# Two cleared PSUM banks and one counting product moved within the experts of a fused attention and mixture kernel

## The chip, the cores and the metric

The kernel runs on one core of one Trainium2 chip. The metric is the device time of one execution in microseconds (us); a kernel's time is the median of its runs.

## What is computed

The reference has three stages: a linear attention with a decaying state, a dense gated layer, and a mixture of eight experts of which each token uses two.

```python
for t in range(S):                       # 4 x 8 heads, 768 steps, head size 48
    state = alpha[:, :, t, :, None] * state + einsum('bhd,bhe->bhde', k[:, :, t], v[:, :, t])
    y[:, :, t] = einsum('bhd,bhde->bhe', q[:, :, t], state)
x = y as 3072 tokens of 384 columns
x = ((x @ w1) * (x @ w2)) @ w3 @ w_out   # 384 -> 1024 -> 1024 -> 384
logits = x @ w_gate + log1p(exp(x @ w_noise)) * noise
top2, weights = the two greatest of 8 experts per token, softmax over them
for e in range(8):
    h = maximum(x[tokens of e] @ w1[e], 0)          # 384 -> 1024
    out[tokens of e] += weight * (h @ w2[e])        # 1024 -> 384
```

## The kernel before

**Stages.** Attention and the dense layer run over eight groups of 384 tokens. Each group ends in `finish` (norms, tokens written to DRAM) and `route` (the two experts of each token), and later `rank` gives each token a slot in its experts' tables. The slots' addresses are `ad` (L697); GpSimd then writes six scatters into the table in DRAM (L700). The experts follow, and this change lies in their beginning.

**An expert** takes 832 slots in two parts of 512 and 320. For a part, SyncE reads the table (`mt`, L971), GpSimd gathers the tokens (`xg`, L910) and SyncE transposes them (`xT`, L916). The first layer runs in eight units (`first`, f = 0 to 7): nine products into one bank (L922 to L924: value and residue in f16), ScalarE takes the positive part (`hh`, L925), VectorE the residue (`hl`, L926), which also frees the bank. The second layer (`second`) runs in tiles of 128 slots, 24 products each (L932 to L934); ScalarE scales the result with the factors `wv` (L976, VectorE, from the table) and GpSimd adds it to the output (L958).

**The last 64 slots** of an expert are not always filled. `count_few` counts the rows of each expert once: it casts the counts `R` to `rb` (L1011), multiplies with ones on TensorE (L1013) and sets a flag per expert, `more` (L1016 to L1018). TensorE loads the flags (L1127) and branches: only where `more` is set, `first_few` runs 72 small products for the last 64 slots (L1038 to L1040), all eight units into one bank. Without those products the bank must hold zeros, so `cleared` has VectorE clear it beforehand (L1027); the products wait for that.

**Banks.** There are eight PSUM banks. A new tile takes the one that was free first by the scheduler's order, and its writer waits for the last reader of the tile before.

**Order.** The kernel is written as one program; a scheduler then sets the order of ScalarE, VectorE, GpSimd and SyncE from its own estimate of durations, while TensorE keeps the order of the code. Each engine runs its queue in that order.

**Around the change** (`experts`): the eight units of expert 0's first part, `rank` of the last group, `count_few`, four tiles of second layers of expert 0's first part, the eight units of expert 1's first part (a table read and transposes beside them), `first_few(0)`, the eight units of expert 0's second part, its tiles, then the eight units of expert 1's second part with `overflow_plan` (a list of slots beyond 832, small steps on VectorE), and `first_few(1)`. For both, `cleared(NF)` stands after unit 4. Weights come in pieces beside all this: load, greatest magnitude (`esc`, L881, then `em`, L884), a product that spreads it (L889), scales (L893 to L897), and a cut into value and residue (`eh` L180, `el` L184).

Of the kernel before, what the change touches and what calls it, by code (L numbers as in the profile page):

```python
# [8 lines left out]
F32 = mybir.dt.float32  # L9
F32R = mybir.dt.float32r  # L10
F16 = mybir.dt.float16
BF = mybir.dt.bfloat16
# [8 lines left out]
P = 128  # L21
# [3 lines left out]
E = 8  # L25
NK = DM // P
NF = F // P
# [54 lines left out]
def body(ctx, tc, q, k, v, alpha, mw1, mw2, mw3, mwo, wg, wn, noise, ew1, ew2, out, dbg=None):  # L82
    nc = tc.nc
# [28 lines left out]
    R = const.tile([P, E], F32, name="R")  # L112
# [92 lines left out]
    def bank(*shape, dt=F32):  # L205

        t = ps.tile([P, PB], F32, name="ps")
        if dt != F32:
            t = t.bitcast(dt)
        n = 1  # L210
        for x in shape:
            n *= x
        t = t[:, :n]
        return t if len(shape) == 1 else t.rearrange("p (a b) -> p a b", a=shape[0])
# [623 lines left out]
    ep = None  # L838
# [89 lines left out]
    def layer2(w2h, w2l, hh, hl, c0, n, mt, wv, t, midway=None, e=None):  # L928
        ts = slice(c0, c0 + n)
        py = bank(DM)  # L930
        for f in range(NF):
            nc.tensor.matmul(py[:n], hh[:, f, ts], w2h[:, f], start=f == 0, stop=False)  # L932
            nc.tensor.matmul(py[:n], hh[:, f, ts], w2l[:, f], start=False, stop=False)  # L933
            nc.tensor.matmul(py[:n], hl[:, f, ts], w2h[:, f], start=False, stop=f == NF - 1)  # L934
            if f == 2 and midway:
                midway()
        put(py[:n], n, mt, wv, t, e)
# [36 lines left out]
    def factors(mt, n, s1, s2, part):  # L974
        wv = ep.tile([P, NTA], F32, name=f"wv{part}")
        nc.vector.tensor_scalar(wv[:, :n], mt[:, :n, 1], s1[:, 4:5], s2[:, 4:5], op0=OP.mult, op1=OP.mult)  # L976
        return wv
# [9 lines left out]
    def fetch_part(e, p):  # L987
        c0, c1 = PARTS[p]
        t0, nt = c0 // P, -(-(c1 - c0) // P)
        rows = P + NTOK - (NL * G if e < NFR and p == 0 else 0)  # L990
        mt = slots(table[e, :, t0:t0 + nt, :], nt, p)
        xT = ep.tile([P, 2 * NK, nt * P], F16, name=f"xT{p}", bufs=1)
        EX[e, p] = (mt, xT, [gather(mt, t, rows) for t in range(nt)])

    def turn_part(e, p, t):
        mt, xT, xg = EX[e, p]
        turn(xg[t], xT, t)

    def first(e, p, f):
        n = PARTS[p][1] - PARTS[p][0]  # L1000
        if (e, p) not in EH:
            EH[e, p] = [ep.tile([P, NF, n], F16, name=f"h{x}{p}", bufs=1) for x in "hl"]
        if p:
            n = FULL - G0
        layer1(f, EW[e][0], EW[e][1], EX[e, p][1], n, *[h[:, :, :n] for h in EH[e, p]])

    def count_few():

        V = nc.vector
        rb = ep.tile([P, E], BF, name="rb", bufs=1)  # L1010
        V.tensor_copy(rb, R)  # L1011
        pc = bank(E)
        nc.tensor.matmul(pc, ones, rb, start=True, stop=True)  # L1013
        n = ep.tile([1, E], F32, name="nf", bufs=1)
        more = ep.tile([1, E], I32, name="more", bufs=1)
        V.tensor_copy(n, pc[0:1])  # L1016
        V.tensor_tensor(n[:, :NFR], n[:, :NFR], skip[0:1], OP.add)
        V.tensor_scalar(more, n, float(FULL), None, op0=OP.is_gt)  # L1018
        return more
# [5 lines left out]
    def cleared(m):  # L1025
        pm = bank(m, CAP - FULL)
        nc.vector.memset(pm, 0.0)  # L1027
        return pm

    def first_few(e, pm):  # L1030
        n, c0 = CAP - FULL, FULL - G0
        w1h, w1l, xT = EW[e][0], EW[e][1], EX[e, 1][1]
        for _ in only_few(e):
            for f in range(NF):
                fs = slice(f * P, (f + 1) * P)
                for kk in range(NK):
                    xh, xl = [xT[:, k, c0:c0 + n] for k in (kk, NK + kk)]
                    nc.tensor.matmul(pm[:, f], w1h[:, kk, fs], xh, start=kk == 0, stop=False)  # L1038
                    nc.tensor.matmul(pm[:, f], w1h[:, kk, fs], xl, start=False, stop=False)  # L1039
                    nc.tensor.matmul(pm[:, f], w1l[:, kk, fs], xh, start=False, stop=kk == NK - 1)  # L1040
        if (e, 1) not in EH:
            EH[e, 1] = [ep.tile([P, NF, CAP - G0], F16, name=f"h{x}1", bufs=1) for x in "hl"]
        hh, hl = [h[:, :, c0:] for h in EH[e, 1]]
        nc.scalar.activation(hh, pm, AF.Relu)
        nc.vector.scalar_tensor_tensor(hl, pm, 0.0, hh, op0=OP.max, op1=OP.subtract)

    def second(e, p, t, midway=None):
        n = PARTS[p][1] - PARTS[p][0]
        mt = EX[e, p][0]
        if t == 0:  # L1050
            WV[e, p] = factors(mt, -(-n // P), EW[e][2], EW[e][5], p)
        wv = WV[e, p]
        layer2(EW[e][3], EW[e][4], *EH[e, p], t * P, min(P, n - t * P), mt, wv, t, midway, e)
# [40 lines left out]
    def next_weights(e):  # L1094
        a, b = weights_for(e)
        todo.extend(pause(1) + a[2:4] + pause(1) + a[5:10] + b[1:2] + a[10:] + pause(1) + b[2:4] + pause(2) + b[5:])

    def prepare(n):

        if not n or not todo:  # L1100
            return
        with ExitStack() as st:
            for e in (mybir.EngineType.DVE, mybir.EngineType.Activation):
                for i in [i for i in nc.cur_bb.bb.instructions[-60:] if i.engine == e][-1:]:
                    st.enter_context(tc.issue_after(i))
            for _ in range(min(n, len(todo))):
                todo.pop(0)()

    def experts():
        for f in range(NF):  # L1110
            first(0, 0, f)
            prepare((0, 1, 1, 1, 1, 1, 1, 1)[f])
        for t in range(NTP[0]):
            turn_part(1, 0, t)
        rank(NG - 1)
        more = count_few()
        for t in range(NTP[0]):
            second(0, 0, t)
            prepare(2)
            if t == 0:  # L1120
                fetch_part(0, 1)
        for f in range(NF):
            first(1, 0, f)
            prepare(1)
            if 0 < f <= NTP[1]:
                turn_part(0, 1, f - 1)
            MORE[f] = nc.tensor.value_load(more[0:1, f:f + 1])  # L1127
            if f == NF // 2:
                pm = cleared(NF)
        first_few(0, pm)  # L1130
        prepare(len(todo))
        fetch_part(1, 1)
        next_weights(2)
        for f in range(NF):
            first(0, 1, f)
            prepare(f // 4)
        for t in range(NTP[1] - 1):
            turn_part(1, 1, t)
            py = cleared(NK) if t else None
            second(0, 1, t)  # L1140
            prepare(2)
        turn_part(1, 1, NTP[1] - 1)
        li = None
        for e in range(1, E):
            if e > 1:
                for f in range(NF):
                    first(e, 0, f)
                    if f == 0:
                        rest = last_few(e - 1, py)
                    if f == 1:  # L1150
                        rest()
                    if f == NF // 2:
                        pm = cleared(NF)
                    prepare(1)
                first_few(e, pm)
            if e + 1 < E:
                fetch_part(e + 1, 0)
            for f in range(NF):
                first(e, 1, f)
                if f == 0 and e == 1:  # L1160
                    rest = last_few(0, py)
                    li = overflow_plan()
                if f == 1 and e == 1:
                    rest()
                if e == 1 and f == NF // 2:
                    pm = cleared(NF)
                prepare(1)
            if e == 1:
                first_few(1, pm)
            if e + 1 < E:  # L1170
                fetch_part(e + 1, 1)
            for t in range(NTP[0]):
                second(e, 0, t)
                prepare(2)
                if e + 1 < E:
                    turn_part(e + 1, 0, t)
            prepare(len(todo))
            if e + 2 < E:
                next_weights(e + 2)
            if e < E - 1:  # L1180
                for t in range(NTP[1] - 1):
                    turn_part(e + 1, 1, t)
                    py = cleared(NK) if t else None
                    second(e, 1, t)
                turn_part(e + 1, 1, NTP[1] - 1)
        py = cleared(NK)
        second(E - 1, 1, 0)
        rest = last_few(E - 1, py)
        second(E - 1, 1, 1, rest)
        return li  # L1190
# [137 lines left out]
```

## Time and profile before

| | us |
|---|---|
| median of 3 runs (lowest, highest) | 947.82 (943.57, 949.92) |
| the profiled execution's own time | 936.92 |
| its span, first to last instruction | 935.1 |
| TensorE busy | 897.5 (96%) |
| VectorE busy | 624.3 (67%) |
| ScalarE busy | 447.6 (48%) |
| GpSimd busy | 259.6 (28%) |

Times in the profile are from the start of the span. PE is TensorE, DVE VectorE, ACT ScalarE, POOL GpSimd, SP SyncE. A row of a timeline has the start, the duration, the engine, the line, the operation with its output and input tiles, and in brackets the idle time before it and what ended it. Matmuls are pipelined: the next one starts before the one before has ended, so the pace is the distance of the starts.

### The profile page before, as it was taken

To read this page: it belongs to the slowest core of one execution; us is meant where nothing else is said; L and a number is where in the kernel's file an instruction comes from. 1 tells how busy PE (TensorE), PEld (TensorE's weight loads), DVE (VectorE), ACT (ScalarE), POOL (GpSimd) and SP (SyncE) were. 2 spreads that over 40 slices of the span, in tenths; PEclk is the share of its full clock that TensorE was granted. 3 is DMA by queue.
4 is the path that set the end of the run, shared out by engine and by line. 5 is a ranking of instruction groups with operands and counts; after the bars stand their busy time and mean duration, and the time that the engine had idled before them with its cause. 6 is when DMAs were issued, how large, how long until landed. Compare 5 with 4: busy or idle time off the path is not lost. (4 is left out here: it accounts for less than half of the span.)

```text
span 935.1 us, 17673 instructions
## 1 busy us (share of the span) xinstructions
PE 897.5 (96%) x6824; PEld 600.0 (64%) x6824; DVE 624.3 (67%) x1733; ACT 447.6 (48%) x916; POOL 259.6 (28%) x246
## 2 busy tenths in 40 slices
PE   7779999999999999999999998999999999999997
PEld 4667777777767666576766455765656564657574
DVE  6899888578788789697769855635555555555320
ACT  2586666364475655754546433334344343434321
POOL 1311110003041131414132243442333333343203
PEclk9889899999999999999999999999999999999999
DMA  9889572241504434101128247585868777776303
GB/s 239 234 148 149 144 200 75 35 93 55 116 10 109 62 102 69 44 26 44 61 83 180 94 87 193 123 165 105 188 122 174 136 155 155 153 157 137 39 10 48
DMA packets 189274, 105.63 MB, mean 113 GB/s; under 512 B 156912, under 2 KB 174912, under 8 KB 189184
## 3 DMA queue, kind: packets, MB, share of 16 engines
q1 hardware_dynamic: 172624, 68.04, 34.2%
q0 software_dynamic: 16560, 36.37, 18.1%
q8 instruction: 59, 0.97, 0.4%
q14 instruction: 31, 0.25, 0.1%
HBM read 73.06 MB, written 20.31 MB: 100 GB/s over the span
## 5 line engine op out<-in xcount | busy, mean ns | idle before, releaser
L958 POOL DMA_INDIRECT out_dram<-ysb,mt x56 | 87.6, 1564 | 151.6 <-ACT ysb L955 147.4
L922 PE MATMUL ps<-xT,eh 128*128 128x256 f16 (+1 forms) x384 | 125.1, 326 | 2.1 <-DVE hl L926 0.9
L934 PE MATMUL ps<-eh,hl 128*128 128x384 f16 x384 | 125.2, 326 | 0.0
L933 PE MATMUL ps<-el,hh 128*128 128x384 f16 x384 | 125.2, 326 | 0.0
L932 PE MATMUL ps<-eh,hh 128*128 128x384 f16 x384 | 125.1, 326 | 0.0
L924 PE MATMUL ps<-xT,el 128*128 128x256 f16 (+1 forms) x384 | 125.1, 326 | 0.0
L923 PE MATMUL ps<-xT,eh 128*128 128x256 f16 (+1 forms) x384 | 125.1, 326 | 0.0
L926 DVE SCALAR_TENSOR_TENSOR hl<-ps,hh 128x512 f16<-128x512 f32 (+1 forms) x128 | 69.7, 552 | 78.8 <-ACT hh L925 78.4
L955 ACT ACTIVATE ysb<-ps,wv 128x384 f32<-128x384 f32 (+1 forms) x56 | 32.4, 579 | 137.9 <-PE ps L934 83.9
L925 ACT ACTIVATE hh<-ps 128x512 f16<-128x512 f32 (+1 forms) x128 | 62.3, 489 | 73.8 <-PE ps L924 65.1
L700 POOL DMA_INDIRECT table<-md,ad x48 | 51.1, 1065 | 154.9 <-DVE ad L697 126.7
L184 DVE SCALAR_TENSOR_TENSOR el<-es,esc,eh 128x512 f16<-128x512 f32 (+1 forms) x80 | 66.7, 851 | 37.8 <-ACT eh L180 37.8
L910 POOL DMA_INDIRECT xg<-x2s,mt x56 | 56.6, 1011 | 95.0 <-DMA mt<-table 59.8
L545 ACT ACTIVATE ab<-ps 128x384 f32<-128x384 f32 (+2 forms) x136 | 63.0, 471 | 36.3 <-PE ps L543 20.8
L182 POOL TENSOR_TENSOR sm<-sf,sm 128x512 f16<-128x512 f32 x24 | 29.8, 1271 | 153.4 <-ACT sm L180 153.4
L541 PE MATMUL ps<-xT,w1h 128*128 128x384 f16 (+2 forms) x204 | 65.2, 321 | 0.9 <-DVE Kt L246 0.6
L541 PE MATMUL ps<-xT,w0h 128*128 128x384 f16 (+2 forms) x204 | 64.9, 320 | 0.9 <-ACT xT L408 0.9
L570 PE MATMUL ps<-Wh,gh 128*128 128x400 f16 x192 | 63.9, 333 | 1.3 <-ACT gh L180 1.1
L543 PE MATMUL ps<-xT,w1l 128*128 128x384 f16 (+2 forms) x204 | 65.1, 320 | 0.0
L542 PE MATMUL ps<-xT,w1h 128*128 128x384 f16 (+2 forms) x204 | 65.1, 320 | 0.0
L543 PE MATMUL ps<-xT,w0l 128*128 128x384 f16 (+2 forms) x204 | 65.0, 320 | 0.0
L542 PE MATMUL ps<-xT,w0h 128*128 128x384 f16 (+2 forms) x204 | 65.0, 320 | 0.0
(303 smaller groups left out, 2083.5 us busy)
## 6 DMA issues: line engine op xcount, KB each, us to landing
es<-in_moe_w_dram SPq DMA_DIRECT2D x32, 768.0 KB, 5.5
s<-in_moe_w_dram POOLq DMA_DIRECT2D x16, 512.0 KB, 4.9
out_dram<-zero POOLq DMA_DIRECT2D x5, 960.0 KB, 5.2
v<-in_v_dram SPq DMA_DIRECT2D x24, 192.0 KB, 2.7
x2s<-xr SPq DMA_DIRECT2D x24, 192.0 KB, 1.9
pad<-in_alpha_dram SPq DMA_DIRECT2D x21, 192.0 KB, 4.0
pad<-in_q_dram SPq DMA_DIRECT2D x21, 192.0 KB, 5.0
pad<-in_k_dram SPq DMA_DIRECT2D x21, 192.0 KB, 4.9
```

Source lines behind the costliest of these rows:

```text
L184: nc.vector.scalar_tensor_tensor(lo, src, scale, hi, op0=OP.mult, op1=OP.subtract)
L541: nc.tensor.matmul(pm, wab[i][0][:, kk, fs], xT[:, kk, cs], start=kk == 0, stop=False)
L542: nc.tensor.matmul(pm, wab[i][0][:, kk, fs], xT[:, NK + kk, cs], start=False, stop=False)
L543: nc.tensor.matmul(pm, wab[i][1][:, kk, fs], xT[:, kk, cs], start=False, stop=kk == NK - 1)
L922: nc.tensor.matmul(pm, w1h[:, kk, fs], xT[:, kk, :n], start=kk == 0, stop=False)
L923: nc.tensor.matmul(pm, w1h[:, kk, fs], xT[:, NK + kk, :n], start=False, stop=False)
L924: nc.tensor.matmul(pm, w1l[:, kk, fs], xT[:, kk, :n], start=False, stop=kk == NK - 1)
L926: nc.vector.scalar_tensor_tensor(hl[:, f], pm, 0.0, hh[:, f], op0=OP.max, op1=OP.subtract)
L932: nc.tensor.matmul(py[:n], hh[:, f, ts], w2h[:, f], start=f == 0, stop=False)
L933: nc.tensor.matmul(py[:n], hh[:, f, ts], w2l[:, f], start=False, stop=False)
L934: nc.tensor.matmul(py[:n], hl[:, f, ts], w2h[:, f], start=False, stop=f == NF - 1)
L958: i = nc.gpsimd.indirect_dma_start(out=out, out_offset=bass.IndirectOffsetOnAxis(ap=mt[:n, t, 0:1].bitcast(U32), axis=0), in_=ys[:n], in_o ...
```

## The change

`count_few` takes its operand `rb` from outside and its product is written behind the first tile of expert 0's second layers instead of before it. The bank of the last 64 slots is cleared after unit 1 instead of after unit 4, for expert 0 and for expert 1.

```diff
-    def count_few():
+    def count_few(rb):
 
         V = nc.vector
-        rb = ep.tile([P, E], BF, name="rb", bufs=1)
-        V.tensor_copy(rb, R)
+        n = ep.tile([1, E], F32, name="nf", bufs=1)
         pc = bank(E)
         nc.tensor.matmul(pc, ones, rb, start=True, stop=True)
-        n = ep.tile([1, E], F32, name="nf", bufs=1)
...
         rank(NG - 1)
-        more = count_few()
+        rb = ep.tile([P, E], BF, name="rb", bufs=1)
+        nc.vector.tensor_copy(rb, R)
         for t in range(NTP[0]):
             second(0, 0, t)
+            if t == 0:
+                more = count_few(rb)
...
-            if f == NF // 2:
+            if f == 1:
                 pm = cleared(NF)
         first_few(0, pm)
...
-                if e == 1 and f == NF // 2:
+                if e == 1 and f == 1:
                     pm = cleared(NF)
```

Lines behind the edit shift by one or two: L1038 is L1036 in the changed kernel, L1027 is L1025.

Since the scheduler takes the code anew, VectorE's order moves in more than the named places. At the end of the last group (narrow products, before `route`), the order of VectorE is, as a difference of changed against before; `esc_7088` is the magnitude of expert 1's second weights, `am` the norms of the last group:

```order
 L881 TENSOR_REDUCE esc_7085<-es 128x1 x2
 L884 TENSOR_REDUCE em<-esc_7085 128x1
-L881 TENSOR_REDUCE esc_7088<-es 128x1
 L172 TENSOR_SCALAR am<-am 128x3
 L173 TENSOR_SCALAR am<-am 128x3
```

The reduction of expert 1's second weights no longer stands before the norms. It stands now behind the slots' addresses `ad` of the last rank and the counting steps, which moved there too; `el_7087` is the residue of expert 1's first weights:

```order
 L694 SCALAR_TENSOR_TENSOR rs<-si 128x6
 L697 TENSOR_TENSOR ad<-rs,rr 128x6
+L1014 COPY nf<-ps 1x8
+L1197 CAST rb<-R 128x8
+L1015 TENSOR_TENSOR nf<-nf,skip 1x2
+L1016 TENSOR_SCALAR more<-nf 1x8
+L881 TENSOR_REDUCE esc_7088<-es 128x1
 L184 SCALAR_TENSOR_TENSOR el_7087<-es,esc_7085,eh_7086 128x512
 L881 TENSOR_REDUCE esc_7088<-es 128x1
```

Four counting steps and one reduction now follow `ad`; before, the counting steps stood between the rank's steps. The third place is VectorE beside expert 1's first units, where `hl_7522` is their residue, `el_7090` the residue of expert 1's second weights and `hl_7718` that of expert 0's last 64 slots:

```order
 L926 SCALAR_TENSOR_TENSOR hl_7522<-ps,hh_7521 128x512
 L184 SCALAR_TENSOR_TENSOR el_7090<-es,esc_7088,eh_7089 128x768
+L1025 MEMSET ps 128x512
 L926 SCALAR_TENSOR_TENSOR hl_7522<-ps,hh_7521 128x512
 L184 SCALAR_TENSOR_TENSOR el_7090<-es,esc_7088,eh_7089 128x768
-L926 SCALAR_TENSOR_TENSOR hl_7522<-ps,hh_7521 128x512
-L1027 MEMSET ps 128x512
-L926 SCALAR_TENSOR_TENSOR hl_7522<-ps,hh_7521 128x512 x4
-L1022 UNCONDITIONAL_BRANCH
-L1045 SCALAR_TENSOR_TENSOR hl_7718<-ps,hh_7717 128x8x64
+L926 SCALAR_TENSOR_TENSOR hl_7522<-ps,hh_7521 128x512 x5
```

The clearing stands one residue of the weights and two of the units earlier. For expert 1 it moved in the same way, from behind the steps of `overflow_plan` to behind the second of them. In TensorE's order only the counting product moved. Of the banks, expert 0's cleared one is now that of the counting product; unit 6 of expert 1 waits for ScalarE in both orders, and unit 7 for VectorE.

## Rows read from the trace of the kernel before

**Rows 1.** The page, busy us, share of the span and instructions of each engine.

```profile
PE 897.5 (96%) x6824; PEld 600.0 (64%) x6824; DVE 624.3 (67%) x1733; ACT 447.6 (48%) x916; POOL 259.6 (28%) x246
```

**Rows 2.** Waits of TensorE, 400 to 935 us: total, times, longest.

```profile
PE ps L1038 <- DVE ps L1027: 3.2, 2, 1.7
PE ps L922 <- DVE hl L926: 0.9, 1, 0.9
PE ps L1013 <- DVE rb L1011: 0.7, 1, 0.7
```

**Rows 3.** Timeline of TensorE: start, us, engine, line, operation.

```profile
541.44 0.17 PE L672 MATMUL ps<-M,ones 128*128 128x24 bf16 x1
...
542.34 0.32 PE L932 MATMUL ps<-eh,hh 128*128 128x384 f16 x1
...
554.03 0.17 PE L889 MATMUL ps<-em,part 128*128 128x1 bf16 x1
...
571.34 0.38 PE L924 MATMUL ps<-xT,el 128*128 128x512 f16 x1
572.62 0.38 PE L922 MATMUL ps<-xT,eh 128*128 128x512 f16 x1 [0.90 <-DVE hl L926]
...
574.35 0.38 PE L924 MATMUL ps<-xT,el 128*128 128x512 f16 x1
576.26 0.19 PE L1038 MATMUL ps<-xT,eh 128*128 128x64 f16 x1 [1.54 <-DVE ps L1027]
...
604.25 0.27 PE L924 MATMUL ps<-xT,el 128*128 128x256 f16 x1
606.18 0.20 PE L1038 MATMUL ps<-xT,eh 128*128 128x64 f16 x1 [1.66 <-DVE ps L1027]
...
840.81 0.38 PE L924 MATMUL ps<-xT,el 128*128 128x512 f16 x1
841.03 0.19 PE L1038 MATMUL ps<-xT,eh 128*128 128x64 f16 x1
```

**Rows 4.** Timeline of VectorE.

```profile
526.07 1.75 DVE L881 TENSOR_REDUCE esc<-es 128x1 f32<-128x1536 f32 x1 [0.72 <-DMA es<-in_moe_w_dram]
527.74 0.16 DVE L172 TENSOR_SCALAR am<-am 128x3 int32<-128x3 int32 x1
...
546.35 0.17 DVE L697 TENSOR_TENSOR ad<-rs,rr 128x6 int32<-128x6 f32 x1
...
550.12 0.16 DVE L884 TENSOR_REDUCE em<-esc 128x1 bf16<-128x2 f32 x1
...
569.83 0.29 DVE L976 TENSOR_SCALAR wv<-mt,esc,esc 128x3 f32<-128x3 f32 x1 [11.31 <-DMA mt<-table]
...
571.89 0.68 DVE L926 SCALAR_TENSOR_TENSOR hl<-ps,hh 128x512 f16<-128x512 f32 x1
...
573.41 0.68 DVE L926 SCALAR_TENSOR_TENSOR hl<-ps,hh 128x512 f16<-128x512 f32 x1
...
575.73 0.48 DVE L1027 MEMSET ps<- 128x512 f32 x1
...
605.64 0.48 DVE L1027 MEMSET ps<- 128x512 f32 x1
```

**Rows 5.** Timeline of ScalarE, the last group's sums of squares.

```profile
526.49 0.19 ACT L575 ACTIVATION_READ_ACCUMULATOR xr<-ps 128x1 f32 x1
```

**Rows 6.** Busy by stretch: PE, PEld, DVE, ACT, POOL, granted clock, DMA share, GB/s.

```profile
527.70:546.50 18.80, 18.10 (x95) 8.88 (x93) 17.60 (x87) 8.88 (x18) 0.00 (x0) 1.00 0.17 54
576.00:578.00 2.00, 1.74 (x60) 1.74 (x60) 2.00 (x5) 0.00 (x0) 0.00 (x0) 1.00 0.91 331
```

**Rows 7.** Timeline of GpSimd, the first of the last six scatters.

```profile
546.79 0.95 POOL L700 DMA_INDIRECT table<-md,ad  x1 [24.55 <-DVE ad L697]
```

**Rows 8.** Timeline of SyncE's queue, the read of the table that L976 waits for.

```profile
565.28 0.57 SPq L971 DMA_DIRECT2D mt<-table  x1
```

**Rows 9.** Operations with tile mt, whole run: time to landing.

```profile
DMA to landing us min/median/max: 1.5/4.4/9.9
```

## The prediction

> **What bounds the kernel.** I read the page first: TensorE is busy 96% of the span [rows 1]. So only time in which TensorE stands still can be won. The list of its waits in the second half (from 400 us) came next. It names three places that this change touches: the product on the last 64 rows waiting for its cleared bank (L1038, 3.2 us in 2), one layer-1 product waiting for a bank (L922, 0.9) and the counting product waiting for its operand (L1013, 0.7) [rows 2]. The list counts from the modelled end of the product before; what TensorE loses is the distance between starts beyond the usual one, so I took the timeline for all four. Counting: L672 starts at 541.44, L932 at 542.34; two small products need 0.03 each (60 of them take 1.74 us [rows 6]), so 0.84 is lost. Unit 7 of expert 1 starts at 572.62, where 571.34 + 0.22 = 571.56 was due: 1.06 lost. The last 64 rows of expert 0 start at 576.26 instead of 574.35 + 0.22 = 574.57: 1.69 lost. Those of expert 1 start at 606.18 instead of 604.25 + 0.11 = 604.36 (256 columns, half of the 0.22 for 512): 1.82 lost [rows 3]. That a taken branch costs nothing of its own is seen at a later expert, whose bank was cleared in time: 840.81 to 841.03, the usual 0.22 [rows 3]. After 606 the list of waits has nothing for TensorE.
>
> Why these waits are there is in VectorE's timeline. It runs in order, and at 569.83 it comes out of an 11.31 us wait for one read of the table (the factors of expert 1's second part, L976) [rows 4]. Behind that stood the residues (hl) of all the units that TensorE had finished meanwhile. I call this moment D. Everything TensorE waits for at 572 and 576 comes at a fixed distance behind D: unit 0's residue starts at D + 2.06, and the clearing starts at 575.73, D + 5.90 [rows 4].
>
> **The counting product.** In the changed order it stands behind the 24 products of the first tile, and its operand is cast long before. TensorE starts the second layers 0.84 us sooner, and the product itself (0.03) is only moved. But this gain alone goes no further than unit 7: that unit needs the bank that unit 0's residue frees, which is set by D. Without an earlier D, TensorE would just wait 0.84 longer there. So I enter nothing for it.
>
> The move adds one wait: VectorE's copy of the counts now waits for a product that ends about 545.5 (541.5 plus 24 products of 0.162; 72 of them lie between 542.34 and 554.03). Queued behind it are one reduction of 1.75 us, the residues of expert 1's first weights, another reduction and the maximum `em`, for which TensorE's product L889 waits. Before, `em` starts at 550.12 and L889 at 554.03 [rows 3, 4], so the cover is 3.9 us; L889 comes 0.84 sooner, and the reduction moved here costs up to 1.75 if no idle time takes it. At least 1.3 us of cover stay, so the cost is nothing; past that, each us is one us of TensorE. The loads of the flag on TensorE come ten us later still.
>
> **What the scheduler moved with it.** That reduction stood before the first step of the last group's norms (L172): it ran from 526.07, and L172 could start only at 527.74 [rows 4]. L172 needs ScalarE's sums, which were there at 526.49 + 0.19 = 526.68 [rows 5]. Now it comes first: about 1.0 us sooner. From there to the slots' addresses (L697) VectorE is busy 17.60 of 18.80 us [rows 6], so it sets the pace there, and the residues between the steps don't wait for TensorE; I take the whole 1.0. The four small counting steps that stood among the rank's steps leave too, but fill the gaps between dependent steps, so I give them 0.05. L697 then comes at 546.35 - 1.05 = 545.30. The bounds are 0 (the residues turn out to wait for TensorE) and 1.4 (all four steps count).
>
> From L697 a chain runs to D with no other late input: GpSimd's six scatters start at 546.79 [rows 7], then the first table read, three gathers, three transposes, and the read that ends D, issued at 565.28 [rows 8]. Each waits for the one before. So D moves from 569.83 to 568.78, and unit 7 from 572.62 to 571.57. **Gain 1.05** (bounds 0 and 1.9, where 1.9 is all that TensorE lost at the first two places).
>
> **Clearing of expert 0.** The clearing moves ahead of the residues of units 1 and 2, to where the residue at 573.41 started [rows 4]: it ends at 573.41 - 1.05 + 0.48 = 572.84. TensorE gets there at 571.57 + 1.94 (nine products of 0.216; eight lie between 572.62 and 574.35) = 573.51, with 0.67 to spare. **Gain 1.69.** The clearing itself costs nothing new: the same 0.48 us, placed earlier. It puts unit 1's residue off by 0.48 (ends 573.5); expert 0's next unit, which takes that bank, starts about 575.6 (573.51 + 72 products of 0.029). The bank is held six units longer. It is the counting product's, long free, and the wait of unit 7 is again for unit 0's residue and that of unit 6 again for ScalarE (order of the changed kernel), so no earlier unit runs out of banks. If one did, unit 6 would wait instead, 1.94 us sooner.
>
> **Clearing of expert 1.** VectorE is full of overflow-plan steps, which stood before the clearing at 605.64 [rows 4]. In the new order it comes behind the second of them, some 6 us sooner, while TensorE comes 2.74 sooner. **Gain 1.82.** The plan is put off by 0.48; what reads it is far from its end.
>
> **Sum.** 1.05 + 1.69 + 1.82 = 4.56 us, from 936.92 (the span of 935.1 and 1.8 around it) to 932.4 in the profiled execution. The runs shown have their median at 947.82, 1.2% above it; the stalls are taken to be the same there: 947.82 - 4.56 = **943.3 us**, 0.5% less.
>
> **A rule weighed.** The granted clock is 1.00, the 2.4 GHz level, in the two us right behind the 1.69 us stall, and 60 small products take 1.74 us there, 0.029 each [rows 6]. The Trainium skill, "TensorE: Matmul & The Clock Gate", section "HAM oscillation — how this bites in real kernels", says that a TensorE left idle between products falls to half its clock and runs the next ones so. By that rule each stall removed would also give back the slow products behind it; the trace shows none slow behind these stalls. As a mechanism of this kernel: 72 products of 0.029 at half rate would be 2.1 us more at either place, so 8.8 us and 939.1 in all.
>
> **Rivals.**
> - *D does not move.* Table reads, gathers and transposes fix it, or VectorE's lead is lost to waits for residues. For: the chain passes GpSimd, SyncE and five DMA landings. Against: each starts when the one before ends. Gain 3.51, 944.3 us.
> - *Given back later.* TensorE comes 4.6 us sooner to experts 2 to 7, and a weight load or gather is then late by as much. For: 96% busy, little else can be wrong. Against: no wait of TensorE after 606, and loads are issued when compute frees their buffers, so they move along. 947.8 us.
> - *Slower: the table read lands late.* D is one DMA, and each us that it lands later costs TensorE one. It took 4.55 us (565.28 to 569.83); operations with this tile took up to 9.9 to land, median 4.4 [rows 9]. Scatters and gathers that start a us sooner could meet the weight loads in another place. At 9.9, D is 5.35 late: 0.8 slower, 948.6 us; it decides from 4.56 us late on. Against: the same transfers stand in the same order around it.
> - *The clock at half rate behind the stalls:* 939.1 us; against it the granted clock of the row.
> - That the clearing isn't moved at all is excluded by the order.
>
> **How the numbers follow.** Forecast 0.63, D unmoved 0.16, given back (some or all) 0.13, table read late 0.04, clock 0.04. About 1% is what a measurement of this kernel can tell from no change: 9.5 us, which no case reaches. The three runs spread from 4.3 below to 2.1 above their median. So the forecast's own range is 939.0 to 945.4; with the given-back and the late case it goes up to 948.6, and down it is left, since the clock case lies inside. Faster by over 1% (below 938.3) only by the spread of the runs: 0.05. Slower by over 1%: 0.02. Same: 0.93.
>
> **What would show it.** Right: the two waits of L1038's successor are gone from TensorE's list; the wait of the counting product too; unit 7 of expert 1 still waits about 0.9 for a residue, but starts about 571.6; VectorE leaves its table wait about 568.8; L172 starts about 526.7; TensorE reaches the second product on 64 rows about 601.6, and the span is about 930.5. Wrong: a wait at unit 6 (banks), at L889 (the reduction), in TensorE's list behind 606 (given back), or the wait at the 64 rows renamed to a transpose of their tokens.

## The result

The changed kernel takes 936.13 us (median of 7 runs, 934.74 to 940.63) against 946.45 us (7 runs, 943.57 to 949.92) for the kernel before. The ratio is 0.9899, 95% interval 0.9877 to 0.9922: 1.0% faster, 9.6 us (1 - 0.9899 of 946.45; gains below are worked out in this way). The prediction said 943.3 us, with 939.0 as the lower end of its range; the measured time lies below that end. A second measurement, with 29 runs of the kernel before beside it, gave 939.02 against 946.57 us, ratio 0.9924 (0.9900 to 0.9949), so 7.2 us. The two intervals overlap between 0.9900 and 0.9922; I take the gain to be 7.4 to 9.5 us, where 4.56 us were forecast.

The profile shown of the changed kernel is of an execution of 934.74 us (span 933.0 us, 1.7 us around it). That is only 2.2 us less than the profiled execution of the kernel before (936.92 us). The two profiles show much less of a gain than the timed executions, and that is what had to be explained.

In the page, TensorE's row is almost that of [rows 1]; the other engines' rows hardly moved either.

```profile
PE 898.9 (96%) x6824; PEld 600.8 (64%) x6824; DVE 624.3 (67%) x1733; ACT 448.2 (48%) x916; POOL 258.3 (28%) x246
```

TensorE's waits from 400 to 935 us (total, times, longest), to be held against [rows 2]: the two waits for a cleared bank and the one of the counting product are gone. The wait of unit 7 for a residue (L922) is still there, as the prediction said. A new entry stands at the head, L889.

```profile
PE ps L889 <- DVE em L884: 1.1, 1, 1.1
...
PE ps L922 <- DVE hl L926: 0.6, 1, 0.6
```

Four starts in TensorE's timeline (start, us, engine, line, operation), to be held against [rows 3]. The changed file is shorter by two lines there, so that L1036 is the old L1038.

```profile
543.84 0.32 PE L932 MATMUL ps<-eh,hh 128*128 128x384 f16 x1
...
573.84 0.38 PE L922 MATMUL ps<-xT,eh 128*128 128x512 f16 x1 [0.59 <-DVE hl L926]
...
575.78 0.19 PE L1036 MATMUL ps<-xT,eh 128*128 128x64 f16 x1
...
604.07 0.19 PE L1036 MATMUL ps<-xT,eh 128*128 128x64 f16 x1
```

This execution came 2.38 us later than the other one to the last group (the unchanged products from about 517 us to 541 us stand that much later in its trace). From there on it catches up: the start of the first second layer at 543.84 stands 1.50 behind 542.34, unit 7 at 573.84 stands 1.22 behind 572.62, the last 64 rows of expert 0 at 575.78 stand 0.48 ahead of 576.26, those of expert 1 at 604.07 stand 2.11 ahead of 606.18. So between the two profiles the change is worth 2.38 + 2.11 = 4.49 us. The forecast for that pair was 4.56.

VectorE's timeline of the changed kernel, to be held against [rows 4]:

```profile
529.10 0.17 DVE L172 TENSOR_SCALAR am<-am 128x3 int32<-128x3 int32 x1 [1.47 <-ACT xr L575]
...
571.05 0.29 DVE L976 TENSOR_SCALAR wv<-mt,esc,esc 128x3 f32<-128x3 f32 x1 [11.10 <-DMA mt<-table]
...
574.82 0.48 DVE L1025 MEMSET ps<- 128x512 f32 x1
...
599.15 0.48 DVE L1025 MEMSET ps<- 128x512 f32 x1
...
602.62 0.42 DVE L926 SCALAR_TENSOR_TENSOR hl<-ps,hh 128x256 f16<-128x256 f32 x1 [2.02 <-ACT hh L925]
```

The step L172 now waits for ScalarE (1.47 us) instead of standing behind the reduction, and VectorE's table wait ends at 571.05. The clearing for expert 1 runs at 599.15. The last row is the clue to what follows: 3.5 us behind the clearing VectorE stands 2.02 us for an activation of ScalarE. In the kernel before, the clearing stood behind that wait.

### The profile page after: what moved, and what is told of

It is laid out like the page before. It is cut to its first block, busy times and chain, and to the rows that moved or that the text cites. A ratio compares the mean times of both kernels' runs of the same rounds, so it can differ in the third digit from the quotient of the medians.

```text
span 933.0 us, 17675 instructions
## 1 busy us (share of the span) xinstructions
PE 898.9 (96%) x6824; PEld 600.8 (64%) x6824; DVE 624.3 (67%) x1733; ACT 448.2 (48%) x916; POOL 258.3 (28%) x246
## 5 line engine op out<-in xcount | busy, mean ns | idle before, releaser
L922 PE MATMUL ps<-xT,eh 128*128 128x256 f16 (+1 forms) x384 | 125.0, 326 | 1.8 <-DVE hl L926 0.6
L910 POOL DMA_INDIRECT xg<-x2s,mt x56 | 54.4, 971 | 99.7 <-DMA mt<-table 64.7
```

Of the source, the lines that this page charges most:

```text
L922: nc.tensor.matmul(pm, w1h[:, kk, fs], xT[:, kk, :n], start=kk == 0, stop=False)
```

## The experiments

Each kernel is timed against the kernel before on the same chip; the ratio stands with its 95% interval.

**The kernel before and the changed kernel again.** No edit. The question was whether the moment at which the kernel before was timed was out of the ordinary, or its profiled execution.

> The kernel before once more, unchanged, timed against itself on the chip of the other three runs. Theory A (the four stalls are all there is, 4.56 us, and the 10.3 us that were measured come from the moment at which the kernel before was timed): ratio 1.000 and times near 937 to 940, as its profiled execution (936.92). Theory B (the kernel before loses about 10 us in most executions, and its profiled execution was a lucky one): ratio 1.000, times near 946, and its new trace has some 6 us more of waits or of lower clock than the trace shown, at a place that the run names.

Measured: 946.25 us, ratio 1.0004 (0.9987 to 1.0020); profiled execution 944.90 us, span 943.0 us. TensorE's waits from 400 to 935 us in it:

```profile
PE ps L1038 <- DVE ps L1027: 5.8, 2, 4.2
PE ps L922 <- DVE hl L926: 1.0, 1, 1.0
```

The wait for the cleared bank is 5.8 us instead of the 3.2 of [rows 2], and its longest is 4.2 instead of 1.7. It is the one of expert 1. VectorE there:

```profile
604.69 0.16 DVE L1208 TENSOR_TENSOR_SCAN oc<-oc 1x8 f32<-1x8 f32 x1
606.71 0.42 DVE L926 SCALAR_TENSOR_TENSOR hl<-ps,hh 128x256 f16<-128x256 f32 x1 [1.87 <-ACT hh L925]
...
611.72 0.16 DVE L1222 TENSOR_SCALAR li<-lst 1x44 int32<-1x44 f32 x1
611.98 0.48 DVE L1027 MEMSET ps<- 128x512 f32 x1
```

VectorE stands 1.87 us for the activation of unit 2; behind it stand all the rest of the overflow plan and at last the clearing, at 611.98. TensorE had started the last product of its units at 608.00. ScalarE in the same place:

```profile
603.31 0.39 ACT L925 ACTIVATE hh<-ps 128x256 f16<-128x256 f32 x1 [0.97 <-PE ps L924]
606.29 0.39 ACT L925 ACTIVATE hh<-ps 128x256 f16<-128x256 f32 x1 [2.60 <-PE ps L924]
```

and the same two activations in the profile shown first, of the kernel before:

```profile
598.46 0.38 ACT L925 ACTIVATE hh<-ps 128x256 f16<-128x256 f32 x1
599.65 0.38 ACT L925 ACTIVATE hh<-ps 128x256 f16<-128x256 f32 x1 [0.80 <-PE ps L924]
```

The two activations stand 2.98 us apart here and 1.19 us there. The profile names a product of TensorE as the releaser, but the products of that unit start at 602.14 and the next unit's at 603.12, so they had long been done. The windows of TensorE tell the second half of the loss (stretch, length, busy us and instructions, granted clock, DMA share, GB/s):

```profile
608.00:610.00 2.00, 0.28 (x3) 1.00 0.18 22
610.00:612.00 2.00, 0.00 (x0) 1.00 0.85 284
612.00:614.00 2.00, 1.48 (x44) 0.90 1.20 232
614.00:616.00 2.00, 2.00 (x34) 0.50 1.46 239
616.00:618.00 2.00, 2.00 (x11) 0.75 1.11 142
618.00:620.00 2.00, 2.00 (x15) 1.00 1.01 340
```

After TensorE stood still, the granted clock falls to 0.50, the 1.2 GHz level, and is back at 1.00 (2.4 GHz) by 618; a mean between the two, such as 0.90 or 0.75, is of a window in which both levels occur. In the profile shown first it stays at 1.00 behind its shorter wait:

```profile
606.00:608.00 2.00, 1.81 (x62) 1.00 1.18 304
608.00:610.00 2.00, 2.00 (x27) 1.00 1.28 229
```

> The changed kernel, timed beside the others on one chip. Theory A: 4 to 5 us below the kernel before, ratio 0.995. Theory B: about 10 us below it, ratio 0.990.

Measured: 939.02 us, ratio 0.9924 (0.9900 to 0.9949). Aligned product by product, its trace gains 1.90 us on the repeat of the kernel before between the second layers of expert 0's first part and the last 64 rows of expert 0, 4.12 us more by those of expert 1, and 1.62 us more by the middle of the second layer's first tile (where the repeat ran at the lower clock). Together 7.64 us, beside 7.2 us by the ratio; another 0.60 us stand ahead of them, where the counting product no longer waits. The ratio lies between the forecasts of the two theories. What speaks for theory B are the 946.25 us of the kernel before and the two traces: the profiled execution of the kernel before was one without most of the loss.

**The parts of the change apart.** Both clearings at unit 1, the counting product left where it was:

```diff
-            if f == NF // 2:
+            if f == 1:
                 pm = cleared(NF)
...
-                if e == 1 and f == NF // 2:
+                if e == 1 and f == 1:
                     pm = cleared(NF)
```

> Only the two clearings move (after unit 1 instead of unit 4); the counting product stays. By the sum: 1.69 + 1.82 = 3.5 us below the kernel before, ratio 0.9963; in the trace the product on the last 64 rows follows the product before it by 0.22 and 0.11 us, the counting product still waits 0.7 for its operand, unit 7 of expert 1 still 0.9. Theory B leaves open which part holds the other 5.7 us: if this one, ratio 0.990.

Measured: 940.47 us, ratio 0.9931 (0.9909 to 0.9954), 6.5 us less. The last 64 rows of expert 1 follow the product before them by 0.11 us as expected, at a clock of 1.00; unit 7 of expert 1 waits 1.4 us instead of 0.9, the counting product 0.4 instead of 0.7. So most of the gain is in the clearings. And the counting product moved alone (`more = count_few(rb)` behind `second(0, 0, 0)`, the cast of `rb` before the loop), the clearings left at unit 4:

> Only the counting product moves, behind the first tile; the clearings stay after unit 4. By the sum: 1.05 us below the kernel before, ratio 0.999; in the trace the first step of the last group's norms no longer stands behind the 1.75 us reduction, the table wait of the vector engine ends about a us sooner against the last unit of expert 0, and the 64 rows of either expert still wait 1.5 to 1.8 for the clearing. If the other 5.7 us are in this part: ratio 0.993.

Measured: 946.28 us, ratio 1.0010 (0.9988 to 1.0033). The counting product's wait is gone from TensorE's list, but the time is that of the kernel before; by the interval at most 1.1 us can be won (0.0012 of 946.6), against 1.05 forecast. The trace shows where one could get lost: at about 514 us it stands 1.30 us behind the repeat of the kernel before, and VectorE's step L697 only 0.56, so 0.74 is won there; but the chain from L697 to the end of VectorE's table wait then takes 24.28 us where it took 23.58. In the thirteen profiles it takes 23.32 to 25.21 us. A gain of 1 us at its head is smaller than its spread. TensorE itself starts the second layers sooner and is 0.58 us better off by their end, and gives 0.53 of it back in unit 7 of expert 1, which waits 1.54 us instead of 1.01, as the prediction says for the case that D does not move. The wait of expert 1's last 64 rows was expected at 1.5 to 1.8 us; it is 3.6.

**The clearings apart.** Only the second expert's at unit 1, then only the first's:

> The kernel before with only the clearing for the second expert (expert 1) at unit 1 instead of unit 4. Theory W (the second place carries the gain: in the repeat of the kernel before TensorE stands there 4.2 us, and its products after that run at a granted clock of 0.50 to 0.75 for some 4 us, 1.3 us more): the stall falls to 0 to 0.3 us and the clock stays at 1.00, gain 5.2 to 5.5 us, about 941.2 us against 946.6. Theory P (the sizes of the recorded prediction, 1.82 us at this place): about 944.8 us. In the trace both want no wait of L1038 at the second expert; only W wants the granted clock unchanged where the repeat of before fell.

Measured: 939.62 us against 945.35 (33 runs), ratio 0.9944 (0.9919 to 0.9970), 5.3 us less. TensorE's list keeps only the wait at expert 0:

```profile
PE ps L1038 <- DVE ps L1027: 1.5, 1, 1.5
```

ScalarE is as late here as in the repeat of the kernel before, but the clearing stands ahead of the step that waits for it, and TensorE's granted clock stays at 1.00 from 606 to 614:

```profile
604.98 0.48 DVE L1027 MEMSET ps<- 128x512 f32 x1
...
607.42 0.38 ACT L925 ACTIVATE hh<-ps 128x256 f16<-128x256 f32 x1 [2.54 <-PE ps L924]
```

> The kernel before with only the clearing for the first expert (expert 0) at unit 1. Theory W: the stall there is 1.6 us in the repeat of before (5.8 us in two waits, the longer 4.2), so the gain is 0.9 to 1.6 us, about 945.3 us, and the second place keeps its wait of about 4 us and its fallen clock. Theory P: 1.69 us, about 944.9. The two agree here; with the run of the other half it tells whether the two gains add up to the 6.1 us of both clearings together.

Measured: 945.73 us, ratio 0.9996 (0.9972 to 1.0019). TensorE's list keeps the wait at expert 1, at its full length:

```profile
PE ps L1038 <- DVE ps L1027: 4.2, 1, 4.2
```

So the second place carries the gain, as theory W says. The first place's gain isn't seen in the time; the interval allows up to 2.6 us (0.0028 of 945.35), the trace loses a wait of 1.54 us there, so nothing contradicts 1.5, but it isn't shown.

**The stall filled.** The kernel before, with work for TensorE while it waits:

```diff
             if e == 1:
+                w1h, xT = EW[1][0], EX[1, 1][1]
+                pf = bank(256)
+                for i in range(28):
+                    nc.tensor.matmul(pf, w1h[:, i % NK, :P], xT[:, i % NK, :256], start=True, stop=True)
                 first_few(1, pm)
```

> The kernel before with 28 more 256-column products (about 3.0 us at 0.109 us each) on TensorE behind unit 7 of the second expert's part 2, into a bank that nobody reads; nothing else is changed. They fill most of the 4.2 us for which TensorE waits for the clearing, so that the 64-row product starts when it did. Theory C (TensorE's own standing still brings the clock down): the granted clock stays at 1.00 through the 64-row product and the second layer behind it, and the time falls by the 1.3 us, to about 945.3. Rival (the rate falls for another reason, such as the branch or the loads of weights behind it): the granted clock falls to 0.5 as before and the time is unchanged, 946.6, or longer by what the filling takes. If the stall is shorter than 3 us in this execution, the filling costs the difference.

Measured: 943.86 us against 945.35, ratio 0.9990 (0.9970 to 1.0010); the time alone doesn't tell 1.3 us from none. The trace does. Its windows behind the filled wait:

```profile
612.00:614.00 2.00, 1.21 (x41) 1.00 1.18 273
614.00:616.00 2.00, 2.00 (x45) 1.00 1.55 193
```

The granted clock stays at 1.00. The first product on 64 rows starts where it did (612.83 here, with 0.79 us of waiting left, 612.52 in the repeat of the kernel before), and a product of the second layer behind it comes 1.6 us nearer. In this kernel:

```profile
612.83 0.20 PE L1038 MATMUL ps<-xT,eh 128*128 128x64 f16 x1 [0.79 <-DVE ps L1027]
...
615.75 0.33 PE L934 MATMUL ps<-eh,hl 128*128 128x384 f16 x1
```

and in the repeat of the kernel before:

```profile
612.52 0.20 PE L1038 MATMUL ps<-xT,eh 128*128 128x64 f16 x1 [4.25 <-DVE ps L1027]
...
617.05 0.33 PE L934 MATMUL ps<-eh,hl 128*128 128x384 f16 x1
```

2.92 us against 4.53 us for the same products: with 28 more products in the wait, those behind it take 1.61 us less. The branch and the loads of weights are the same in both, so it is TensorE's own standing still that brought the clock down. This rests on one trace with the filling; the traces without it are counted further down.

**The plan behind the clearing.** The clearing stays at unit 4, and the plan of the overflow goes behind it:

```diff
                 if f == 0 and e == 1:
                     rest = last_few(0, py)
-                    li = overflow_plan()
...
                 if e == 1 and f == NF // 2:
                     pm = cleared(NF)
+                if e == 1 and f == NF // 2:
+                    li = overflow_plan()
```

> The kernel before with the clearing for the second expert left at unit 4 and the plan of the overflow (its product that counts rows and the 13 small VectorE steps) moved from unit 0 to behind that clearing. On VectorE the clearing then stands right behind the third of the eight units' steps. Theory V (the clearing is late because the plan's chain stands ahead of it on VectorE and waits with it for ScalarE's late activation): the clearing runs about 0.4 us behind that step, some 4.5 us sooner than in the repeat of before, TensorE's wait at the second place and the fallen clock go, about 941.2 us. Rival (what is late is ScalarE alone, and VectorE's chain only follows it): the clearing stays late by 2 to 4 us and the gain is under 2 us, 944.6 to 946.6.

Measured: 940.96 us, ratio 0.9949 (0.9926 to 0.9973), 4.8 us less. VectorE in this kernel:

```profile
605.38 0.42 DVE L926 SCALAR_TENSOR_TENSOR hl<-ps,hh 128x256 f16<-128x256 f32 x1 [1.79 <-ACT hh L925]
605.91 0.48 DVE L1027 MEMSET ps<- 128x512 f32 x1
```

ScalarE is late here too (1.79 us of VectorE's time), but the clearing comes right behind the residue that waits for it, where in the repeat of the kernel before thirteen steps stand between the two, eight of them of the plan; the clearing runs at 605.91 instead of 611.98 and TensorE's wait at expert 1 is gone. What made the clearing late is the plan's chain that stands ahead of it in VectorE's order and stops with ScalarE. The run doesn't part the two cleanly: ScalarE's activation of unit 2 stands 2.97 us ahead of the product on 64 rows here (604.97 and 607.94), and 1.82 us ahead of that product's due start in the repeat of the kernel before (606.29 and 608.11), so it also comes some 1.1 us sooner. But with the 5.27 us that lie between residue and clearing in that repeat (606.71 to 611.98), the clearing would still run at 605.38 + 5.27 = 610.65, and TensorE would wait some 3 us (an estimate). Clearing at unit 1 is one way out, putting the plan behind is another; the two can't be told apart in time.

**ScalarE's gap.** Its activations of units 1 and 2 follow a conditional branch (around the second layer of expert 0's last 64 rows). The kernel before without that branch:

```diff
-        for _ in only_few(e):
+        for _ in only_few(e) if e else (0,):
             for k in range(NK):
```

> The kernel before without the conditional branch around the second layer of the first expert's last 64 rows (the 72 products are always done; in this input they are done anyway). The clearing for expert 1 stays behind the plan at unit 4. In six of seven profiles in which the plan stands ahead of the clearing or the clearing stands early, ScalarE stands 2.5 to 2.6 us between its activations of units 1 and 2 after this branch, with TensorE's product long done. Theory S (what holds ScalarE comes with leaving the branch): the 2.5 us go, the clearing runs about 2.5 us sooner, TensorE waits about 1.6 us instead of 4.2 at the second place, the granted clock stays at 1.00 behind it, and the time falls by about 4 us, to 941.5 to 942.5 against 945.5 to 946.5. Rival: ScalarE stands there all the same and the time is that of before within 1 us.

Measured: 942.24 us against 945.62 (17 runs), ratio 0.9973 (0.9952 to 0.9995), 2.6 us less. ScalarE in the same place:

```profile
602.80 0.38 ACT L925 ACTIVATE hh<-ps 128x256 f16<-128x256 f32 x1 [0.95 <-PE ps L924]
603.59 0.58 ACT L955 ACTIVATE ysb<-ps,wv 64x384 f32<-64x384 f32 x1 [0.41 <-PE ps L924]
605.04 0.38 ACT L925 ACTIVATE hh<-ps 128x256 f16<-128x256 f32 x1 [0.87 <-PE ps L924]
```

The gap of 2.6 us is now in pieces (0.41 and 0.87, with another step between them), and the two activations are 2.24 us apart instead of 2.98. TensorE's wait at expert 1 falls to 2.0 us, and still the clock falls behind it:

```profile
610.00:612.00 2.00, 2.00 (x50) 0.59 1.29 154
612.00:614.00 2.00, 2.00 (x27) 0.56 1.89 226
```

Theory S is half right: the branch's going takes 2.3 us off the wait (4.25 to 1.98), but ScalarE is late without it, and the order of its steps changed a little too. What holds ScalarE there stays open. No packet of the instruction queues lies in the gap in the three traces of the kernel before that have it, so that they show no cause either.

**Two more executions of the kernel before.**

> The kernel before once more, for the spread of its wait at the second place. The theory that most executions have the long wait: L1038's longest wait is about 4.2 us and the granted clock behind it falls below 1.00. If the profile shown first was an ordinary one: about 1.7 us and 1.00.

> As the other look: a longest wait of L1038 of about 4.2 us with a fallen clock behind it, if the long wait is the ordinary case; about 1.7 us and a clock of 1.00 if the profile shown first was.

Measured: 946.76 and 942.89 us. Both have the long wait, the first and then the second:

```profile
614.73 0.23 PE L1038 MATMUL ps<-xT,eh 128*128 128x64 f16 x1 [4.24 <-DVE ps L1027]
```

```profile
610.64 0.23 PE L1038 MATMUL ps<-xT,eh 128*128 128x64 f16 x1 [4.16 <-DVE ps L1027]
```

and the clock behind it in the second:

```profile
610.00:612.00 2.00, 1.36 (x26) 0.63 1.20 276
612.00:614.00 2.00, 2.00 (x43) 0.52 1.06 217
```

So three of the four profiles of the kernel before have a wait of 4.2 us and the lower clock behind it. The one shown first is the exception, and its 936.92 us is less than any of the 86 timed runs of the kernel before that stand beside these measurements (lowest 941.16).

Aligned product by product with the profile shown first, the three others lose 4.0 to 4.5 us between 596 and 617 us, at this place. Another 1.8 to 5.8 us stand ahead of it, most of them between 435 and 526 us, before anything that the change moves; why the executions differ there is not explored.

Over all thirteen profiles, the clock falls behind each wait of expert 1's last 64 rows of 1.98 to 4.25 us (six profiles), and the next 95 products then take 7.12 to 7.48 us; in the other seven, with waits of up to 1.66 us, they take 5.84 or 5.85. So the lower clock costs 1.3 to 1.6 us. The length of a wait alone does not decide it. In the first of the two executions, unit 7 of expert 1 waits 2.62 us and the clock stays at 1.00:

```profile
578.39 0.38 PE L922 MATMUL ps<-xT,eh 128*128 128x512 f16 x1 [2.62 <-DVE hl L926]
```

```profile
578.00:580.00 2.00, 1.61 (x8) 1.00 0.75 186
```

and in the trace with only expert 1's clearing at unit 1 it falls behind a wait of 1.91 us, at another place:

```profile
514.40 0.18 PE L889 MATMUL ps<-em,part 128*128 128x1 bf16 x1 [1.91 <-DVE em L884]
```

```profile
516.00:518.00 2.00, 2.00 (x8) 0.50 0.00 0
```

What else decides is not shown by these runs.

## Why the prediction was wrong, point by point

- **Where TensorE loses time, and what the change does to it: right.** The three waits that it named are gone, unit 7 keeps its own, nothing new stands behind 606.
- **The counting product (0 by itself, 1.05 through VectorE's order): right between the two profiles, not seen in the time.** L172 waits for ScalarE instead of the reduction, as worked out, and D, the end of the table wait, stands 1.22 behind that of before where 2.38 was due: 1.16 gained. That it comes so near to 1.05 is luck in part, since the chain in between varies by 1.9 us from trace to trace. Alone the part gave nothing that can be measured. The cover of the added wait held: the product L889 that could have suffered has no wait. The 1.1 us at the head of the new list belong to another L889, at 512 us, ahead of everything that the change touches; the kernel before has 0.7 to 1.6 us there in its three other profiles.
- **Clearing of expert 0 (1.69): right between the two profiles** (1.22 behind becomes 0.48 ahead, 1.70), and within what its own run allows.
- **Clearing of expert 1 (1.82): this is the step that failed.** Between the two profiles it is 1.63, but in ordinary executions of the kernel before the wait is 4.2 us and the products behind it run at the lower clock for 1.6 us more. The term is 5 to 6 us: 5.3 measured with that clearing alone, 4.12 + 1.62 = 5.74 in the traces. The sentence that carried the mistake is "the stalls are taken to be the same there": it added the profile's 4.56 to runs that were 10.9 us slower than the profile, without asking where these 10.9 us were. In the repeat of the kernel before, 8.0 us slower than the profile, 4.2 of the 8.0 are at this very place (4.25 - 1.66 more wait, and 1.6 behind it), and nearly all of the rest lies ahead of the change.
- **The rule that was weighed and put at 0.04: wrong to dismiss.** The row behind the 1.69 us wait shows a granted clock of 1.00 [rows 6], and so does the row behind the 1.66 us wait at expert 1. Behind 4.2 us of standing still it falls to 0.50. The Trainium skill, "TensorE: Matmul & The Clock Gate", section "HAM oscillation — how this bites in real kernels", says that a TensorE which stands idle between bursts starts the next one at half its clock. The traces agree behind the waits of 1.98 to 4.25 us at expert 1, and the filled stall shows it by undoing it; behind the wait of 2.62 us at unit 7 they do not. One row that doesn't show a rule at work said nothing of the same place with a longer wait.
- **The range.** Its lower end of 939.0 held the spread of the runs and the clock at both places (939.1), but no longer stall. The wait at expert 1 was priced from one execution alone, so its size had no bound upward.

With the terms as measured, 1.5 (expert 0, by the trace) + 4.2 + 1.6 (expert 1, wait and clock) + 0.5 (the counting product's own wait, 0.4 to 0.7 in the other profiles of the kernel before), the sum is 7.8 us. Of these terms only expert 1's is seen in a time of its own. The sum is near the second measurement (7.2 us) and lies inside the first one's interval (7.4 to 11.6 us); that the first one's middle is 9.6 isn't explained.

## What to carry to other kernels

When the profiled execution is faster than every timed run, the difference is a term of its own: look for the wait that may be longer in the ordinary run before adding a gain worked out from the fast one. A small job that another engine will wait for should not stand in an in-order engine behind a chain that itself waits for a third engine; its lateness is then the sum of both. And a wait of TensorE has to be priced with the products behind it, whose clock the trace of a shorter wait doesn't show.

## What was not expected of the hardware

- TensorE's granted clock fell from 1.00 to 0.50 behind waits of 1.98 to 4.25 us at one place and of 1.91 us at another, and not behind waits of 1.54, 1.66 and, once, 2.62 us. With the wait of 4.2 us filled down to 0.79 us it stayed at 1.00, and the products behind were 1.6 us faster.
- ScalarE stood 2.5 to 2.6 us between two activations of the same kind in ten of the thirteen profiles, at the same pair of instructions each time, in the repeat of the kernel before with its operand ready and nothing in the trace that ends the gap. Removing a branch ahead of it broke the gap up and shortened it, and moving the plan did so too; the cause is not known.
